# Chunked attention, top-2 routing and experts on one core: the attention as a four-stage pipeline, with the routing cut into single steps

## The chip, the cores and the metric

One Trainium2 chip, of which the kernel uses one core. The metric is the device time of one execution in microseconds. TensorE multiplies (PE in the profile, its weight loads PEld), VectorE is DVE, ScalarE is ACT, GpSimd is POOL, SyncE is SP. Each engine runs its own instructions in order and waits for others by semaphores. DMAs are issued by POOL, SP or ACT and run on 16 DMA engines of the core.

## The reference

Two steps. First attention over batches b = 0..3, 8 heads, 768 positions, head size 64: each chunk of 32 positions sees 16 positions to its left, its own 32, 8 to its right, and 8 memory positions:

```
k_full = concat([mem_k, k[l_start:r_end]]); v_full likewise
scores = (q_c @ k_full.T) / 8
a = softmax(scores)
out[chunk] = a @ v_full
```

Then the outputs, as 3072 tokens of 512 numbers, go through a mixture of 8 experts with noise on the routing:

```
noisy = x @ w_gate + log1p(exp(x @ w_noise)) * noise
top2, their softmax weights g
out[n] = sum over the two experts e of g * (relu(x @ w1[e]) @ w2[e])
```

## The kernel before, in words

**Attention.** A head pair n (0 to 15; four per batch) is two heads side by side on 64 partitions each. `load_group` (L253) fetches q, k and v for two pairs at once; there are eight such groups and three buffers. POOL issues the q, k and v DMAs (L261, L274 to L280); SP issues the memory rows of v (L282) and the blank rows of the scatter target (L87). For one pair:

- `qkT` (L333): TensorE transposes q and k in 12 steps of 128x128 f32 (L342), ACT casts them to bf16 (L343), POOL copies the edges of k by 16 and 8 columns (L344, L345), so that each chunk sees a window of 56 columns.
- `scores` (L348): 48 matmuls of a chunk's 32 queries with its 56 keys (L356), then 48 with the 8 memory keys (L362), on array tiles of 64x32; VectorE takes maximum and difference (L367, L369), ACT the exponential (L370).
- `probT` (L373): six transposes (L377) and a copy out of PSUM by VectorE (L379).
- `cast_v` (L285): v is cast to bf16 by POOL for even pairs and VectorE for odd ones (L290), with two edge chunks scaled (L292).
- `mix` (L384): 48 matmuls with v (L394), VectorE divides by the sum (L398, L399) into the batch's row buffer `xrow`, two of which take turns.

The loop (L406) runs `qkT(n+2)`, `probT(n)`, `scores(n+1)`, `mix(n)`, `cast_v(n+1)`. After each second `qkT` it asks for the group two further on.

**Routing.** `dispatch` (L126) follows each batch by one pair. For 6 tiles of 128 tokens it transposes the rows (L133), ACT copies them (L135), TensorE makes 16 logits (L137). Then some 35 small VectorE operations (L142 to L224) find the two best experts, the rank of each token in its pair of experts (with sums by TensorE, L173 to L177 and L191 to L195, over `seen` of the batches before) and its slot (L204). POOL scatters the rows to `x_by_pair` in DRAM in 6 indirect DMAs (L227). The routing of the last batch comes after the loop.

**Experts.** The 28 pairs of experts have 128 slots each. SP reads the rows back (L487, L490, L450) when all scatters have landed; POOL issues the expert weights (L437, L438; two experts' are buffered), TensorE does both matmuls (L512, L547), ACT and VectorE evict, POOL scatters the output (L554). A loop over spilled rows behind it runs only where a pair of experts got more than 128 tokens and 32 spill rows are used up.

**What sets the order.** The kernel's text gives a priority to each instruction, and a scheduler puts them in one fixed order per engine when the kernel is built, where it may move an instruction ahead of others that wait. What the order holds is therefore read from the built kernel; on each engine it is kept on the chip. PSUM has 8 banks: scores 2, transposes 3, mixes 2, routing 1.

Of the kernel before, what the change touches and what calls it, by code (L numbers as in the profile page):

```python
# [12 lines left out]
F32 = mybir.dt.float32  # L13
# [8 lines left out]
def kernel(  # L22
# [102 lines left out]

    def dispatch(b, xrow):  # L126
        T = lambda name, shape, dt=F32: rpool.tile(shape, dt, name=name)
        t0 = b * BT
        ps_l = psR.tile([128, BT, 2 * E], F32, name="ps_l", tag="rt")
        for t in range(BT):  # L130
            p_x = psT.tile([128, KP, 128], BF16, name="p_x", tag="tr")
            for kp in range(KP):
                nc.tensor.transpose(out=p_x[:, kp, :], in_=xrow[:, t, kp * 64:(kp + 1) * 64].bitcast(BF16), identity=identb)  # L133
            xt = rpool.tile([128, KP, 128], BF16, name="xt")
            nc.scalar.copy(xt, p_x)  # L135
            for kp in range(KP):
                nc.tensor.matmul(out=ps_l[:, t, :], lhsT=xt[:, kp, :], rhs=wgn[:, kp, :], start=(kp == 0), stop=(kp == KP - 1))  # L137
        ns = T("ns", [128, BT, E])
        nc.scalar.activation(out=ns, in_=ps_l[:, :, E:], func=Act.Exp)
        nc.scalar.activation(out=ns, in_=ns, func=Act.Ln, bias=1.0)  # L140
        nl = T("nl", [128, BT, E])
        nc.vector.tensor_mul(nl, ns, nz_all[:, t0:t0 + BT, :])  # L142
        nc.vector.tensor_tensor(out=nl, in0=nl, in1=ps_l[:, :, :E], op=Alu.add)

        codeb = code.rearrange("p (o e) -> p o e", o=1).to_broadcast([128, BT, E])
# [4 lines left out]
        for i, src in enumerate((nl, nl2)):  # L150
            nc.vector.tensor_reduce(out=m[i], in_=src, axis=AX, op=Alu.max)
            nc.vector.tensor_tensor(out=eq, in0=src, in1=bc(m[i], E), op=Alu.is_equal)
            nc.vector.tensor_mul(eq, eq, codeb)
            nc.vector.tensor_reduce(out=c[i], in_=eq, axis=AX, op=Alu.max)
            if i == 0:
                nc.vector.tensor_tensor(out=eq, in0=codeb, in1=bc(c[0], E), op=Alu.is_equal)
                nc.vector.scalar_tensor_tensor(out=nl2, in0=eq, scalar=-1e30, in1=nl, op0=Alu.mult, op1=Alu.add)

        cM, cm = T("cM", [128, BT]), T("cm", [128, BT])
        nc.vector.tensor_max(cM, c[0], c[1])  # L160
        nc.vector.tensor_tensor(out=cm, in0=c[0], in1=c[1], op=Alu.min)
        pa, pb, pos = T("pa", [128, BT]), T("pb", [128, BT]), T("pos", [128, BT])
        nc.vector.tensor_scalar(out=pa, in0=cM, scalar1=float(E - 1), scalar2=None, op0=Alu.mult)
        nc.vector.scalar_tensor_tensor(out=pa, in0=cm, scalar=-float(E), in1=pa, op0=Alu.mult, op1=Alu.add)
        nc.vector.tensor_scalar(out=pb, in0=cM, scalar1=-float(E), scalar2=float(E * E), op0=Alu.mult, op1=Alu.add)
        nc.vector.scalar_tensor_tensor(out=pb, in0=cm, scalar=float(E - 1), in1=pb, op0=Alu.mult, op1=Alu.add)
        nc.vector.tensor_tensor(out=pos, in0=pa, in1=pb, op=Alu.min)

        oh = T("oh", [128, BT, NB], BF16)
        nc.vector.tensor_tensor(out=oh, in0=ramp.rearrange("p (o e) -> p o e", o=1).to_broadcast([128, BT, NB]),  # L170
                                in1=bc(pos, NB), op=Alu.is_equal)
        ps_r = psR.tile([128, BT, NB], F32, name="ps_r", tag="rt")
        nc.tensor.matmul(out=ps_r, lhsT=upper, rhs=oh, start=True, stop=False)  # L173
        for t in range(1, BT):
# [3 lines left out]
                         start=False, stop=True)  # L178
        sums = T("sums", [128, NB])
        nc.vector.tensor_reduce(out=sums, in_=oh.rearrange("p t e -> p e t"), axis=AX, op=Alu.add)  # L180
        nc.vector.tensor_add(seen, seen, sums)

        rk = T("rk", [128, BT, NB])
        rank = T("rank", [128, BT])
        nc.vector.tensor_tensor(out=rk, in0=oh, in1=ps_r, op=Alu.mult)
        nc.vector.tensor_reduce(out=rank, in_=rk, axis=AX, op=Alu.add)

        ov = T("ov", [128, BT], BF16)
        nc.vector.tensor_scalar(out=ov, in0=rank, scalar1=float(CAP), scalar2=None, op0=Alu.is_ge)
        ps_o = psR.tile([128, BT + 1], F32, name="ps_ov", tag="rt")  # L190
# [4 lines left out]
        nc.tensor.matmul(out=ps_o[:, :BT], lhsT=ones, rhs=seen_ov.to_broadcast([128, BT]), start=False, stop=True)  # L195
        ov1 = T("ov1", [128, 1])
        nc.vector.tensor_reduce(out=ov1, in_=ov, axis=AX, op=Alu.add)
        nc.vector.tensor_add(seen_ov, seen_ov, ov1)
        slot, spl = T("slot", [128, BT]), T("spl", [128, BT])
        nc.vector.scalar_tensor_tensor(out=slot, in0=pos, scalar=float(CAP), in1=rank, op0=Alu.mult, op1=Alu.add)  # L200
        nc.vector.scalar_tensor_tensor(out=spl, in0=ps_o[:, :BT], scalar=float(NB * CAP), in1=slot, op0=Alu.add, op1=Alu.subtract)
        nc.vector.tensor_mul(spl, spl, ov)
        slot_i = rpool.tile([128, BT], I32, name="slot_i")
        nc.vector.tensor_tensor(out=slot_i, in0=slot, in1=spl, op=Alu.add)  # L204

        ex, g1, g2 = T("ex", [128, BT]), T("g1", [128, BT]), T("g2", [128, BT])
        nc.vector.tensor_sub(ex, m[1], m[0])
        nc.scalar.activation(out=ex, in_=ex, func=Act.Exp)
        nc.vector.tensor_scalar(out=g1, in0=ex, scalar1=1.0, scalar2=None, op0=Alu.add)
        nc.vector.reciprocal(g1, g1)  # L210
        nc.vector.tensor_mul(g2, ex, g1)
        first = T("first", [128, BT])
        nc.vector.tensor_tensor(out=first, in0=c[0], in1=c[1], op=Alu.is_gt)
        dg = T("dg", [128, BT])
        nc.vector.tensor_sub(dg, g1, g2)
        nc.vector.tensor_mul(dg, dg, first)

        meta = xrow[:, :, XC:].bitcast(F32)
        nc.vector.tensor_copy(meta[:, :, 0:1], tok_i[:, t0:t0 + BT].rearrange("p (t o) -> p t o", o=1))
        o1 = lambda ap: ap.rearrange("p (t o) -> p t o", o=1)  # L220
        nc.vector.tensor_tensor(out=meta[:, :, 1:2], in0=o1(g2), in1=o1(dg), op=Alu.add)
        nc.vector.tensor_tensor(out=meta[:, :, 2:3], in0=o1(g1), in1=o1(dg), op=Alu.subtract)
        nc.vector.tensor_copy(meta[:, :, 3:4], o1(cM))
        nc.vector.tensor_copy(meta[:, :, 4:5], o1(cm))  # L224
        nc.gpsimd.memset(meta[:, :, 5:8], 0.0)
        for t in range(BT):
            nc.gpsimd.indirect_dma_start(  # L227
                out=xd_tile[t0 + t], out_offset=bass.IndirectOffsetOnAxis(ap=slot_i[:, t:t + 1], axis=0),
                in_=xrow[:, t, :], in_offset=None, bounds_check=NROW - 1, oob_is_err=True)
        if b == B - 1:  # L230
            nc.tensor.matmul(out=ps_o[:, BT:BT + 1], lhsT=ones, rhs=seen_ov, start=True, stop=True, skip_group_check=True)
            nc.vector.tensor_copy(n_spill, ps_o[:, BT:BT + 1])
            nc.vector.tensor_scalar(out=n_spill_i, in0=ps_o[:, BT:BT + 1], scalar1=float(SPILL), scalar2=None, op0=Alu.max)


    actx = ExitStack()
    apool = actx.enter_context(tc.tile_pool(name="apool", bufs=2))
    psS = actx.enter_context(tc.psum_pool(name="psS", bufs=1))
    psT = actx.enter_context(tc.psum_pool(name="psT", bufs=3))
    psA = actx.enter_context(tc.psum_pool(name="psA", bufs=1))  # L240
    psR = actx.enter_context(tc.psum_pool(name="psR", bufs=1))
# [8 lines left out]
    PADL, PADR = left_ctx, right_ctx  # L250
# [34 lines left out]
    def cast_v(n):  # L285
# [3 lines left out]
        eng = nc.vector if n % 2 else nc.gpsimd  # L289
        eng.tensor_copy(vw[:, 1:ncnk - 1, 0:D], vf[:, hp % HV, 1:ncnk - 1, :])  # L290
        for c, col in ((0, live[:, 0:1]), (ncnk - 1, live[:, 1:2])):
            eng.tensor_scalar(out=vw[:, c, 0:D], in0=vf[:, hp % HV, c, :], scalar1=col, scalar2=None, op0=Alu.mult)  # L292
# [40 lines left out]
    def qkT(n):  # L333
        b, hp = divmod(n, HP)
        qn, kn, _ = groups_in[b, hp // HV]
        qT = apool.tile([128, S], BF16, name="qT", bufs=3)
        kT = apool.tile([128, PADL + S + PADR], BF16, name="kT", bufs=3)
        for src, dst, o in ((qn, qT, 0), (kn, kT, PADL)):
            for g in range(2):
# [3 lines left out]
                nc.scalar.copy(dst[:, o + g * HT * 128:o + (g + 1) * HT * 128], p_t)  # L343
        nc.gpsimd.tensor_copy(kT[:, :PADL], kT[:, PADL:2 * PADL])  # L344
        nc.gpsimd.tensor_copy(kT[:, PADL + S:], kT[:, S + PADL - PADR:S + PADL])  # L345
        st[n].update(qT=qT, kT=kT)

    def scores(n):  # L348
        b, hp = divmod(n, HP)
        qT, kT = st[n]["qT"], st[n]["kT"]  # L350
        ps = [psS.tile([128, BT, CTX], F32, name=f"ps_s{hh}") for hh in range(2)]
        for c in range(ncnk):
            u, r = divmod(c, 4)
            for hh in range(2):
                hs = slice(64 * hh, 64 * hh + 64)
                nc.tensor.matmul(out=ps[hh][32 * r:32 * r + 32, u, :WIN], lhsT=qT[hs, chunk * c:chunk * (c + 1)],  # L356
                                 rhs=kT[hs, chunk * c:chunk * c + WIN], start=True, stop=True)
        for c in range(ncnk):
            u, r = divmod(c, 4)
            for hh in range(2):  # L360
# [283 lines left out]
```

## Time and profile before

| | us |
|---|---|
| median of 3 timed runs (lowest, highest) | 483.78 (481.44, 484.1) |
| profiled execution | 479.79 |
| its span | 478.0 |
| TensorE busy in the span | 322.1 (67%) |
| VectorE, ACT, POOL busy | 171.6, 127.4, 165.2 |

A row of a timeline is: start in us from the span's start, duration in us, engine, line, operation, output<-inputs, shapes, count of instructions merged into the row, and in brackets the engine's idle time just before it with what ended it. "issue" there means that nothing the profile shows was waited for. A row of the windows is: from:to, length, then for PE, PEld, DVE, ACT, POOL the busy time and the number of instructions, then the granted TensorE clock as a share of full speed, the share of the time for which the DMA engines were busy, and the GB/s that they moved. "to landing" is the time from a DMA's issue to its completion.

### The profile page before, as it was taken

The numbers are of one execution on the slowest core, as the hardware profiler recorded it, in microseconds if no ns is written. First come the engines' busy times: TensorE is split into PE (matmuls) and PEld (weight loads), VectorE is DVE, ScalarE is ACT, GpSimd is POOL, SyncE is SP. The second block draws the span as 40 slices with busy tenths as digits, with TensorE's granted clock in tenths as the row PEclk, the third lists the DMA queues.
The fourth block names the chain that finished last, engine by engine and source line by source line (L and its number), as shares of the span: only waits on it lengthen the run. The fifth ranks groups of instructions, "written<-read, shape, count | busy, mean of one in ns | idle before, by whom it ended". The sixth has DMA issues, their size and how long they took to land. (4 is left out here: it accounts for less than half of the span.)

```text
span 478.0 us, 10565 instructions
## 1 busy us (share of the span) xinstructions
PE 322.1 (67%) x4481; PEld 199.1 (42%) x4497; DVE 171.6 (36%) x493; ACT 127.4 (27%) x233; POOL 165.2 (35%) x267
## 2 busy tenths in 40 slices
PE   2225555454555484510399599599899999999992
PEld 2114444344444363400254265264455545454541
DVE  1014437565346468440230231231324323333341
ACT  2212232623352244500033123132231223131200
POOL 9756562179317810651100100200303140313133
PEclk9999985965556566555599789899999999999998
DMA  7999998139922800299315615715835665761112
GB/s 136 261 294 282 293 224 178 48 99 209 237 55 86 203 6 3 71 191 226 86 33 90 121 36 88 137 30 88 172 61 123 100 148 87 161 110 73 40 57 86
DMA packets 41842, 60.06 MB, mean 126 GB/s; under 512 B 14170, under 2 KB 29623, under 8 KB 41792
## 3 DMA queue, kind: packets, MB, share of 16 engines
q0 software_dynamic: 23008, 49.93, 47.0%
q1 hardware_dynamic: 18464, 9.35, 8.9%
q8 instruction: 37, 0.61, 0.6%
q14 instruction: 13, 0.11, 0.1%
q10 hardware_dynamic: 320, 0.07, 0.1%
HBM read 62.73 MB, written 14.47 MB: 162 GB/s over the span
## 5 line engine op out<-in xcount | busy, mean ns | idle before, releaser
L512 PE MATMUL ps_h<-xTb,w1t 128*128 128x384 bf16 (+4 forms) x832 | 112.8, 292 | 1.0 <-DVE xTb L454 1.0
L547 PE MATMUL ps_y<-w2t,ht 128*128 128x512 bf16 x432 | 97.1, 379 | 0.9
L512 PEld LDWEIGHTS <-w1t 128*128 128x128 bf16 x832 | 62.0, 99 | 44.3 <-issue 3.7
L516 ACT ACTIVATE ht<-ps_h 128x512 bf16<-128x512 f32 x64 | 38.2, 597 | 133.6 <-PE ps_h L512 133.6
L547 PEld LDWEIGHTS <-ht 128*128 128x128 bf16 x448 | 43.2, 98 | 51.5
L518 DVE TENSOR_SCALAR ht<-ps_h 128x416 bf16<-128x416 f32 x64 | 37.9, 592 | 65.2 <-PE ps_h L512 65.2
L554 POOL DMA_INDIRECT out_dram<-acc,tid x28 | 28.1, 1003 | 78.4 <-DVE acc L553 41.0
L553 DVE SCALAR_TENSOR_TENSOR acc<-ps_y,meta,acc 128x512 f32<-128x512 f32 x28 | 21.0, 751 | 54.5 <-PE ps_y L547 54.5
L227 POOL DMA_INDIRECT x_by_pair<-xrow,slot_i x24 | 24.5, 1023 | 37.3 <-DVE vwin L292 15.1
L551 ACT ACTIVATE acc<-ps_y,meta 128x512 f32<-128x512 f32 x28 | 19.2, 687 | 61.3 <-PE ps_y L547 61.3
L342 PE MATMUL p_t<-ident,qn 128*128 128x128 f32 x96 | 22.5, 393 | 13.8 <-DMA qn<-in_q_dram 11.8
L370 ACT ACTIVATE P<-sd 128x384 bf16<-128x384 f32 x32 | 15.7, 522 | 54.4 <-DVE sd L369 54.4
L343 ACT CAST qT<-p_t 128x384 bf16<-128x384 f32 x32 | 15.1, 479 | 42.8 <-PE p_t L342 42.4
L356 PE MATMUL ps_s<-kT,qT 64*32 64x56 bf16 x768 | 13.9, 219 | 16.7 <-POOL kT L344 5.7
L437 POOL DMA_DIRECT2D w1t<-in_moe_w_dram x8 | 6.4, 801 | 54.1 <-PE ps_h L512 54.1
L280 POOL DMA_DIRECT2D vf<-in_v_dram x16 | 22.8, 1426 | 6.2 <-issue 5.6
L342 PE MATMUL p_t<-ident,kn 128*128 128x128 f32 x96 | 21.0, 380 | 5.6 <-DMA kn<-in_k_dram 5.6
L455 POOL COPY meta<-xl 128x8 f32<-128x8 f32 x28 | 5.3, 190 | 55.7 <-DMA xl<-x_by_pair 55.6
L367 DVE TENSOR_REDUCE mx<-ps_s 128x6 f32<-128x384 f32 x32 | 16.4, 550 | 21.6 <-PE ps_s L362 18.8
L453 PE MATMUL p_t<-identb,xl 128*128 128x128 bf16 x112 | 13.0, 250 | 15.3 <-DMA xl<-x_by_pair 10.5
L342 PEld LDWEIGHTS p_t<-ident,qn 128*128 128x128 f32 x96 | 16.3, 203 | 15.3 <-issue 12.5
L362 PE MATMUL ps_s<-mkT,qT 64*32 64x8 bf16 x768 | 10.4, 176 | 16.8 <-issue 16.8
(139 smaller groups left out, 379.3 us busy)
## 6 DMA issues: line engine op xcount, KB each, us to landing
vf<-in_v_dram POOLq DMA_DIRECT2D x14, 672.0 KB, 14.4
w1t<-in_moe_w_dram POOLq DMA_DIRECT2D x8, 1024.0 KB, 8.4
w2t<-in_moe_w_dram POOLq DMA_DIRECT2D x8, 1024.0 KB, 11.1
qn<-in_q_dram POOLq DMA_DIRECT2D x14, 384.0 KB, 11.8
kn<-in_k_dram POOLq DMA_DIRECT2D x14, 384.0 KB, 11.8
x_by_pair<-blank SPq DMA_DIRECT2D x1, 3696.0 KB
xl<-x_by_pair SPq DMA_DIRECT2D x28, 132.0 KB
vf<-in_mem_v_dram SPq DMA_DIRECT2D x32, 48.0 KB
```

The lines of the kernel that those rows point to most:

```text
L227: nc.gpsimd.indirect_dma_start(out=xd_tile[t0 + t], out_offset=bass.IndirectOffsetOnAxis(ap=slot_i[:, t:t + 1], axis=0), in_=xrow[:, t, :] ...
L280: nc.gpsimd.dma_start(out=dst[:, lo:hi, :], in_=src(lo, hi - lo))
L342: nc.tensor.transpose(out=p_t[:, t * 128:(t + 1) * 128], in_=src[:, hp % HV, g * HT + t, :, :], identity=ident)
L367: nc.vector.tensor_reduce(out=mx, in_=ps[hh], axis=AX, op=Alu.max)
L370: nc.scalar.activation(out=P[:, :, hh, :], in_=sd, func=Act.Exp, scale=scale)
L512: nc.tensor.matmul(out=ps_h[:, off:off + n], lhsT=w1t[:, kp, f * 128:(f + 1) * 128], rhs=rhs(kp), start=(kp == 0 and i == 0), stop=(kp == ...
L516: nc.scalar.activation(out=ht[:, f, lo:hi], in_=ps_h[:, :hi - lo], func=Act.Relu)
L518: nc.vector.tensor_scalar(out=ht[:, f, lo:hi], in0=ps_h[:, :hi - lo], scalar1=0.0, scalar2=None, op0=Alu.max)
L547: nc.tensor.matmul(out=ps_y, lhsT=ht[:, f, j * CAP:(j + 1) * CAP], rhs=w2t[:, f, :], start=(f == 0), stop=(f == FB - 1))
L551: nc.scalar.activation(out=acc[p], in_=ps_y, func=Act.Copy, scale=gate)
L553: nc.vector.scalar_tensor_tensor(out=acc[p], in0=ps_y, scalar=gate, in1=acc[p], op0=Alu.mult, op1=Alu.add)
L554: nc.gpsimd.indirect_dma_start(out=out_tile[p], out_offset=bass.IndirectOffsetOnAxis(ap=tid[p][:, 0:1], axis=0), in_=acc[p], in_offset=Non ...
```

## The change

It has six parts, all ahead of the experts.

- The loop is a pipeline of four stages: in step n, `qkT(n)`, `scores(n-1)`, `probT(n-2)` with `cast_v(n-2)`, `mix(n-3)`. A group is asked for as soon as the second `qkT` of the group three before it is through.
- `dispatch` is a generator. `tick()` runs it on to its next `yield`; it is called 10 times per pair, between the VectorE operations of the pair. A routing has 59 such steps and joins the list of jobs when its batch's last `mix` is through. What is left after the loop is run off there.
- POOL issues DMAs only: the 56 columns of the edge chunks are made by two matmuls each (`context`) in place of the copied edges of k, and v is cast by ACT for every pair, its edges scaled by VectorE. The column of zeros in the row buffer is set once, at the start.
- There are three row buffers, made once, in place of two.
- In the scores the context matmul and the memory matmul of a chunk and head stand one behind the other, where there were 48 and then 48.
- PSUM: 3 banks for transposes and all routing results, 5 shared by scores and mixes. The six tiles' logits are copied out to `lg` one by one, and the copies of the transposed rows are shared by VectorE and ACT.

The diff, cut to its core (the many `V.` lines of the routing are the same operations as before, with a `yield` between them, some in another order):

```diff
     def dispatch(b, xrow):
...
         for t in range(BT):
             p_x = psT.tile([128, KP, 128], BF16, name="p_x", tag="tr")
             for kp in range(KP):
                 nc.tensor.transpose(...)
-            xt = rpool.tile([128, KP, 128], BF16, name="xt")
-            nc.scalar.copy(xt, p_x)
+            yield
+            xt = rpool.tile([128, KP, 128], BF16, name="xt", bufs=3)
+            (nc.scalar.copy if t % 2 else V.tensor_copy)(xt, p_x)
+            yield
+            ps_l = psT.tile([128, 2 * E], F32, name="ps_l", tag="tr")
             for kp in range(KP):
-                nc.tensor.matmul(out=ps_l[:, t, :], ...)
+                nc.tensor.matmul(out=ps_l, ...)
+            yield
+            V.tensor_copy(lg[:, t, :], ps_l)
+            yield
...
+    def tick(n=1):
+        for _ in range(n):
+            while jobs:
+                try:
+                    next(jobs[0])
+                    break
+                except StopIteration:
+                    jobs.pop(0)
...
-    psS = actx.enter_context(tc.psum_pool(name="psS", bufs=1))
     psT = actx.enter_context(tc.psum_pool(name="psT", bufs=3))
-    psA = actx.enter_context(tc.psum_pool(name="psA", bufs=1))
-    psR = actx.enter_context(tc.psum_pool(name="psR", bufs=1))
+    psW = actx.enter_context(tc.psum_pool(name="psW", bufs=5))
...
     def cast_v(n):
-        eng = nc.vector if n % 2 else nc.gpsimd
-        eng.tensor_copy(vw[:, 1:ncnk - 1, 0:D], vf[:, hp % HV, 1:ncnk - 1, :])
+        nc.scalar.copy(vw[:, 1:ncnk - 1, 0:D], vf[:, hp % HV, 1:ncnk - 1, :])
         for c, col in ((0, live[:, 0:1]), (ncnk - 1, live[:, 1:2])):
-            eng.tensor_scalar(...)
+            V.tensor_scalar(...)
...
     def qkT(n):
...
-        nc.gpsimd.tensor_copy(kT[:, :PADL], kT[:, PADL:2 * PADL])
-        nc.gpsimd.tensor_copy(kT[:, PADL + S:], kT[:, S + PADL - PADR:S + PADL])
...
     def scores(n):
-        ps = [psS.tile([128, BT, CTX], F32, name=f"ps_s{hh}") for hh in range(2)]
+        ps = [psW.tile([128, BT, CTX], F32, name="ps_s", tag="w") for _ in range(2)]
         for c in range(ncnk):
             for hh in range(2):
-                nc.tensor.matmul(out=ps[hh][32 * r:32 * r + 32, u, :WIN], lhsT=qT[hs, ...], rhs=kT[hs, ...], ...)
-        for c in range(ncnk):
-            for hh in range(2):
-                nc.tensor.matmul(out=ps[hh][32 * r:32 * r + 32, u, WIN:], lhsT=qT[hs, ...], rhs=mkT[hs, ...], ...)
+                for a, z, t in context(kT, hs, c):
+                    nc.tensor.matmul(out=o[:, a:z], lhsT=ql, rhs=kT[hs, t:t + z - a], start=True, stop=True)
+                nc.tensor.matmul(out=o[:, WIN:], lhsT=ql, rhs=mkT[hs, hp, b * n_mem:(b + 1) * n_mem], ...)
...
+    for i in range(3):
+        xr = rcon.tile([128, BT, ROW], I32, name=f"xrow{i}")
+        nc.gpsimd.memset(xr[:, :, XC:], 0)
...
+        if hp == HP - 1:
+            jobs.append(dispatch(b, xrows[b % 3]))
...
-    qkT(0)
-    qkT(1)
-    scores(0)
-    cast_v(0)
-    for n in range(NPAIR):
-        b, hp = divmod(n, HP)
-        if n + 2 < NPAIR:
-            qkT(n + 2)
-        if (n + 2) % HV == HV - 1 and (n + 2) // HV + 2 < len(GR):
-            load_group(*GR[(n + 2) // HV + 2])
-        probT(n)
-        if n + 1 < NPAIR:
-            scores(n + 1)
-        mix(n)
-        if n + 1 < NPAIR:
-            cast_v(n + 1)
-        if n == 0:
-            fill_blank()
-        if hp == 0 and b > 0:
-            dispatch(b - 1, xrows[b - 1])
-    dispatch(B - 1, xrows[B - 1])
+    for n in range(NPAIR + 3):
+        if n < NPAIR:
+            qkT(n)
+            if n % HV == HV - 1 and n // HV + 3 < len(GR):
+                load_group(*GR[n // HV + 3])
+        tick()
+        if 0 <= n - 1 < NPAIR:
+            scores(n - 1)
+        if 0 <= n - 2 < NPAIR:
+            probT(n - 2)
+            cast_v(n - 2)
+        if 0 <= n - 3 < NPAIR:
+            mix(n - 3)
+        if n == 2:
+            fill_blank()
+    while jobs:
+        tick()
```

## The prediction

> **What bounds the kernel now.** The page's chain of waits is of no use here: it stops after one piece, the last output DMA. So I read the table of windows first, cut where the stages change, then the timelines of POOL, of TensorE and of the hand-over to the experts. The profiled execution took 479.79 us, its span 478.0; the median of the three timed runs is 483.78, 4.0 us more. I work in the profiled execution and carry the difference to the median at the end.
>
> The windows, with each engine's busy time, the granted clock, the share of DMA time and GB/s:
>
> ```profile
> 37.00:82.00 45.00, 23.91 (x863) 19.88 (x863) 22.69 (x51) 12.08 (x28) 23.81 (x35) 0.84 1.02 253
> 82.00:126.00 44.00, 23.26 (x719) 19.36 (x716) 24.30 (x87) 17.18 (x37) 26.54 (x33) 0.66 0.57 137
> 126.00:170.00 44.00, 21.98 (x591) 18.78 (x588) 21.00 (x78) 15.36 (x31) 21.36 (x30) 0.54 0.50 120
> 170.00:195.00 25.00, 16.62 (x581) 12.86 (x581) 19.43 (x83) 11.87 (x23) 2.94 (x7) 0.64 0.02 4
> ...
> 237.40:478.00 240.60, 218.89 (x1615) 114.70 (x1628) 70.93 (x124) 57.46 (x92) 46.92 (x87) 0.95 0.45 92
> ```
>
> The experts start at 237.4 us and keep TensorE busy for 218.9 of 240.6 us. The change touches nothing there, so I carry that stage unchanged and look only at when it starts. Ahead of it no engine is over 60% busy, and DMA is full only until 82 us. Two things waste the time. First, POOL's queue is in order, and a scatter that waits for its slots holds up the loads behind it:
>
> ```profile
> 88.72 1.11 POOL L261 DMA_DIRECT2D qn<-in_q_dram  x1 [0.16 <-issue]
> 96.72 1.24 POOL L227 DMA_INDIRECT x_by_pair<-xrow,slot_i  x1 [6.89 <-DVE vwin L292]
> ...
> 104.38 1.10 POOL L261 DMA_DIRECT2D qn<-in_q_dram  x1
> ```
>
> The load begun at 88.72 goes on at 104.38, 14.6 us after its first part ended; the same happens at 135.53 (on at 152.72). The last group's loads thus leave POOL at 159.3. Second, TensorE, when it has work, stands still with no releaser:
>
> ```profile
> 44.66 0.26 PE L362 MATMUL ps_s<-mkT,qT 64*32 64x8 bf16 x20 [2.64 <-issue]
> ...
> 52.50 0.24 PE L356 MATMUL ps_s<-kT,qT 64*32 64x56 bf16 x6 [3.03 <-issue]
> ...
> 59.18 0.25 PE L356 MATMUL ps_s<-kT,qT 64*32 64x56 bf16 x16 [2.61 <-issue]
> ```
>
> In the packed trace each of these stops holds one 16 KB packet of the instruction queue (37 packets in all), and they lie 256 TensorE instructions apart: code loading, 2.8 us each while DMA is full. Last, the hand-over: the last routing block's slots, its last scatter, the first read of the scattered rows, the first expert matmul:
>
> ```profile
> 208.73 0.16 DVE L204 TENSOR_TENSOR slot_i<-slot,spl 128x6 int32<-128x6 f32 x1
> ...
> 216.22 0.98 POOL L227 DMA_INDIRECT x_by_pair<-xrow,slot_i  x1 [0.30 <-issue]
> ...
> 228.18 0.32 SPq L487 DMA_DIRECT2D s_x<-x_by_pair  x1
> ...
> 237.46 1.06 PE L512 MATMUL ps_h<-xTb,w1t 128*128 128x512 bf16 x2
> ```
>
> I call T the end of the last pair's sd on VectorE, 190.5 us (L369). From T to the experts there are 47 us.
>
> **Part by part.** I price T' (T in the changed kernel), then the tail from T'.
>
> *POOL issues only.* The kT edge copies (32 at 0.2 us) and half the V casts (8 at 1.37 us and 16 edges at 0.44) leave POOL. In the built order all five remaining load groups stand ahead of the first scatter, each waiting only for its buffers. So the 14.6 and 16.1 us holes go. What is late next? The bytes: eight groups of 3.07 MB (0.77 q, 0.77 k, 1.34 v, 0.19 memory rows) and 3.7 MB of blanks, 28.3 MB; at the 253 GB/s of 37 to 82 us that is 112 us. Two pairs behind the last landing T' would be about 128: the floor.
>
> *V cast on ACT.* The trace has no such cast. ACT's rows 128x384 (479 ns) and 128x512 (597) give 118 ns per 128 columns, so 128x1408 takes about 1.4 us (VectorE 0.89, POOL 1.37 for the same): 16 of them 23 us on an ACT that is busy 56.5 of the 158 us from 37 to 195. It waits for vf, behind it the next pairs' qT casts; the vf of a group lands before the q of the next, so I charge nothing; the bound is one vf landing, 13.8 us (median), once.
>
> *VectorE.* 16 more edge scalings (0.25), 12 xt copies (0.42, as L454's equal shape), 24 logit copies (0.16), less 8 casts (0.89): +5.8 us on 87.4 busy of 158. Hidden beside TensorE.
>
> *TensorE's own work.* Busy from 37 to 195 us: 85.8 us. Of that the changed order puts before 32 us (scores of pairs 0 and 1, no longer queued behind pair 2's transposes) 1.9 us, and behind T' routing 2 (4.9, as the window of 195 to 217 has for routing 3), the end of routing 1 (1.3) and the last two pairs' transposes and mixes (2.9). Left: 74.8 us. The granted clock fell to 0.54 without making this work longer per matmul (27.7 ns a matmul in 37:82, 28.6 in 170:195), so I take it as it stands.
>
> *Code loading* is not removed: the instruction number stays (64 matmuls more). Between 42 and 195 us the trace has 22 packets; some 19 fall between 32 us and T'. About 12 of them come while the loads still fill DMA, at 2.8 to 3 us: 35 us. The other 7 at some 0.7 us (in 170:195, with DMA empty, TensorE stops of that kind are below 1.3 us): 5 us. The Trainium skill (Runtime: NRT & Kernel Launch, Instruction fetch mechanics) calls the crossing of a 16 KiB block "mostly hidden". By that T' would fall to the DMA floor; the three rows above speak against it where DMA is full.
>
> *The pipeline and the five shared PSUM buffers.* L356 x43 then x5 shows the scores waiting for their single buffer; with five, softmax is taken from a pair earlier. I take these waits as gone but for 3 us.
>
> T' = 32 (k of pairs 2 and 3 arrives at 31.8, L342) + 74.8 + 40 + 3 = **150**.
>
> *Routing spread out.* One step is made per tick: 59 steps per routing, 10 ticks per pair. So a routing takes almost six pairs, four routings need 236 ticks, and from the first routing on the loop has only 111. The rest is drained after the last pair. The built VectorE order shows it: after the last sd come the second half of routing 1, the multiplications of the last four pairs (they wait for scatter 0 to free the row buffer), all of routing 2, then all of routing 3. From T':
> - end of routing 1: second selection to slots 6.2 us (89.45 to 95.64), two PT copies and edges 1.7: 7.9
> - three tiles of routing 2's logits 3, four multiplications 2.2, mixes of 14 and 15 3.4: 16.5
> - rest of routing 2: logits 2.5, exp, table load and log 1.8 (199.55 to 201.34), chain 7.5 (201.35 to 208.9): 28.3
> - routing 3: logits 4.5 (195.03 to 199.5) and six copies 1, then 1.8 and 7.5: 43.1
> - six scatters 8.4 (slots to 217.2), landing 2.9: 54.4
> - first read to first matmul 9.3 (228.18 to 237.46): 63.7.
>
> Before, the scatter had landed only at 228, 11 us after its issue, beside four weight loads issued at 201 to 205. Now three of these are issued at about T'+17 and, at some 8 us each (8.4 and 11.1 to landing), are in by T'+45, so I take the 2.9. The bound is those 8 us again.
>
> So the tail grows from 47 to 64, +17; T falls by 40.5. Sum: -23.5 us. 479.8 - 23.5 = 456.3 in the profiled execution, 460.3 against the median; I say **458**.
>
> **The rivals.**
> *A, code loading is hidden after all* (loads come earlier and smoother, so its packets pass): T' = 128 + 6 for the last routing steps, experts at 198, 440 against the profile. For it: 9 of 22 packets cost nothing in the trace; against it: those nine came while TensorE waited for something else.
> *B, slower: two score matmuls in a row on one array tile.* The changed loop issues, for each chunk and head, the context matmul and at once the memory matmul on the same 64x32 tile; now 48 of one kind run over eight tiles in turn. The order is not in the trace. Below: nothing (96 in 0.95 us from 37.25 to 38.20, 10 ns each, L356 and L362). Above: as L193, five on one tile in 0.27 us, 54 ns each: 48 x 44 ns = 2.1 us per pair, 14 pairs, +30: 486. It decides from 1.6 us per pair, where the 23.5 us are used up. I take nothing, since operand shapes are those of L356 and L362, but keep the end. The Trainium skill (TensorEngine Tiling (Array Packing), Tiling Modes) says that different tiles can load and multiply in parallel, which promises nothing for one tile twice.
> *C, it doesn't do what it says:* the pairs keep nearly their pace (11 us per pair from 82 to 170) because code loading and in-order waits for routing steps fill the holes. Of the 40 us T loses only 15 to 22: 474 to 482. For it: TensorE busy plus 2.9 us per packet is already 39 of every 44 us.
>
> **Chances.** Forecast 0.56 (own range 446 to 470: 12 packets at 2 to 4 us, weights in the way or not); A 0.14; B 0.12; C 0.14; other 0.04. The range leaves out B and the far ends of A and C: 438 to 480. A measurement here tells about 0.5%, 2.4 us. Faster by more: forecast, A, most of C: 0.80. Within: 0.06. Slower: B and a little of C: 0.14.
>
> **What would show it.** Right: POOL's loads without the 15 us holes, the last group issued near 100 us; T' near 150 with TensorE stops of 2 to 4 us and no releaser, most before 110; two routings one behind the other between the last mix and the last scatter, some 27 us; experts near 214, then 240 us as before. Wrong: a T' near 130 (A), score blocks of over 2.5 us per pair (B), T' past 170 (C), or an expert stage of another length.

## The result, and the profile of the changed kernel

The changed kernel takes 507.08 us (median of 4 runs, 504.0 to 515.7), the kernel before 482.61 in the same comparison: 1.0495 of it, 95% interval 1.041 to 1.058. It is slower, by about what it was forecast to gain, and outside the range. The profiled execution is the slowest of the four, 515.7 us with a span of 513.9, so its rows hold some 9 us more than the median; a second profile (below), of 513.8 us, has the same rows.

First the windows, 10 to 60 us, while loads fill DMA in both kernels (columns as in the prediction: PE, PEld, DVE, ACT, POOL, clock, DMA share, GB/s). Before:

```profile
10.00:60.00 50.00, 20.22 (x517) 16.38 (x518) 12.14 (x30) 11.12 (x25) 31.21 (x38) 1.00 1.08 277
```

After:

```profile
10.00:60.00 50.00, 19.40 (x558) 15.78 (x558) 10.69 (x25) 13.09 (x24) 23.31 (x24) 0.89 1.08 215
```

DMA is as busy (1.08) and moves 22% less. The page's list of DMA issues (KB each, median us from issue to landing) says the same. Before, these loads landed after 14.4 us (v) and 11.8 (q and k); now:

```profile
vf<-in_v_dram POOLq DMA_DIRECT2D x14, 672.0 KB, 21.5
...
qn<-in_q_dram POOLq DMA_DIRECT2D x14, 384.0 KB, 19.9
kn<-in_k_dram POOLq DMA_DIRECT2D x14, 384.0 KB, 21.6
```

Next SP's queue. The memory rows of v for pairs 4 and 5 (the `x4`) are issued behind the blank write (L87). Before, SP is through with them at 62.9 us:

```profile
9.26 0.66 SPq L87 DMA_DIRECT2D x_by_pair<-blank  x1
9.96 52.95 SPq L282 DMA_DIRECT2D vf<-in_mem_v_dram  x4
```

After, at 97.9:

```profile
10.24 2.90 SPq L87 DMA_DIRECT2D x_by_pair<-blank  x1
13.19 84.68 SPq L319 DMA_DIRECT2D vf<-in_mem_v_dram  x4
```

Who waits for these rows is in the timelines of ACT, TensorE and POOL:

```profile
114.46 2.63 ACT L326 CAST vwin<-vf 128x1408 bf16<-128x1408 f32 x2 [33.14 <-DMA vf<-in_mem_v_dram]
```

```profile
58.08 0.19 PE L402 MATMUL ps_s<-mkT,qT 64*32 64x8 bf16 x1 [6.41 <-issue]
...
85.65 0.50 PE L441 MATMUL ps_o<-vwin,PT 64*32 64x65 bf16 x34 [6.85 <-issue]
...
117.53 0.90 PE L378 MATMUL p_t<-ident,kn 128*128 128x128 f32 x3 [29.27 <-ACT qT L379]
...
132.58 0.19 PE L402 MATMUL ps_s<-mkT,qT 64*32 64x8 bf16 x1 [7.91 <-issue]
```

```profile
117.54 2.81 POOL L317 DMA_DIRECT2D vf<-in_v_dram  x2 [24.37 <-DMA vf<-in_mem_v_dram]
...
143.90 2.81 POOL L317 DMA_DIRECT2D vf<-in_v_dram  x2 [19.06 <-ACT kT L379]
```

ACT stands 33 us at the V cast of pair 4, the casts of q and k wait behind it, and TensorE and then POOL wait for those. The other three PE rows are stops with an instruction packet in them: 6.4 to 7.9 us, where the three rows of this kind in the prediction have 2.6 to 3.0. They stand inside blocks of scores and mixes whose first matmuls are already through. The hand-over, from DVE, POOL, SP and PE in turn:

```profile
211.15 0.55 DVE L412 TENSOR_TENSOR sd<-ps_s,mx 128x384 f32<-128x384 f32 x1
...
253.81 0.17 DVE L250 TENSOR_TENSOR slot_i<-slot,spl 128x6 int32<-128x6 f32 x1
```

```profile
260.75 0.98 POOL L254 DMA_INDIRECT x_by_pair<-xrow,slot_i  x1 [0.30 <-issue]
```

```profile
263.44 0.32 SPq L534 DMA_DIRECT2D s_x<-x_by_pair  x1
```

```profile
272.60 1.49 PE L559 MATMUL ps_h<-xTb,w1t 128*128 128x512 bf16 x3
```

T' (end of the last sd) is 211.7 us, not 150; from there the experts start 60.9 us later (forecast: 63.7) and take 241.3 (before: 240.5). So the whole miss lies ahead of T'. The table adds up the time from 32 us to T'. TensorE's idle stretches of over 1 us are sorted by whether an instruction packet falls into them (packed trace); shorter ones count as other waits.

| us | before | prediction | after | e13, load buffers moved (below) |
|---|---|---|---|---|
| start | 32 | 32 | 32 | 32 |
| TensorE's own work | 84.5 | 74.8 | 75.4 | 73.6 |
| stops with an instruction packet | 33.0 | 40 | 52.7 | 37.7 |
| the stop behind ACT's V cast | none | 0 | 29.3 | 11.2 |
| all other waits | 41.6 | 3 | 22.3 | 16.0 |
| end of the last sd | 191.1 | 150 | 211.7 | 170.5 |

### The profile page after: what moved, and what is told of

Same layout as the page of the kernel before. It is cut to its first block, busy times and chain, and to the rows that moved or that the text cites. A ratio compares the mean times of both kernels' runs of the same rounds, so it can differ in the third digit from the quotient of the medians.

```text
span 513.9 us, 10712 instructions
## 1 busy us (share of the span) xinstructions
PE 322.8 (63%) x4561; PEld 198.2 (39%) x4561; DVE 171.3 (33%) x537; ACT 142.9 (28%) x237; POOL 138.5 (27%) x210
## 5 line engine op out<-in xcount | busy, mean ns | idle before, releaser
L378 PE MATMUL p_t<-ident,kn 128*128 128x128 f32 x96 | 23.1, 392 | 48.9 <-ACT qT L379 41.1
L378 PEld LDWEIGHTS p_t<-ident,kn 128*128 128x128 f32 x96 | 16.8, 204 | 52.0 <-ACT qT L379 43.3
L326 ACT CAST vwin<-vf 128x1408 bf16<-128x1408 f32 x16 | 21.0, 1359 | 36.2 <-DMA vf<-in_mem_v_dram 33.1
L378 PE MATMUL p_t<-ident,qn 128*128 128x128 f32 x96 | 23.7, 415 | 10.7 <-DMA qn<-in_q_dram 10.7
L402 PE MATMUL ps_s<-mkT,qT 64*32 64x8 bf16 x768 | 18.6, 173 | 17.3 <-issue 17.3
L401 PE MATMUL ps_s<-kT,qT 64*32 64x56 bf16 (+3 forms) x832 | 20.5, 202 | 13.1 <-issue 11.9
L441 PE MATMUL ps_o<-vwin,PT 64*32 64x65 bf16 x768 | 11.8, 219 | 23.8 <-issue 23.8
L402 PEld LDWEIGHTS <-qT 64*32 64x32 bf16 x768 | 15.6, 100 | 19.5 <-issue 19.1
L298 POOL DMA_DIRECT2D qn<-in_q_dram x18 | 18.1, 1006 | 17.6 <-PE p_t L378 10.3
```

Of the source, the lines that this page charges most:

```text
L326: nc.scalar.copy(vw[:, 1:ncnk - 1, 0:D], vf[:, hp % HV, 1:ncnk - 1, :])
L378: nc.tensor.transpose(out=p_t[:, t * 128:(t + 1) * 128], in_=src[:, hp % HV, g * HT + t, :, :], identity=ident)
L401: nc.tensor.matmul(out=o[:, a:z], lhsT=ql, rhs=kT[hs, t:t + z - a], start=True, stop=True)
L402: nc.tensor.matmul(out=o[:, WIN:], lhsT=ql, rhs=mkT[hs, hp, b * n_mem:(b + 1) * n_mem], start=True, stop=True)
```

## The experiments

These are the theories, in the order in which they came. Theory 1: the memory rows of v come late because they stand behind the blank write, and the cast's place on ACT makes it worse. Theory 2: code loading in a full DMA is the loss. Theory 3, after the second profile: the load packets themselves got slower. In the packed trace the mean load packet takes 202 ns in the first 10 us before the change and, in the second profile, 299 after it, at the same size (304 in the first profile); over the first 60 us it is 204 against 262 to 266. What differs is where the packets go. In the built kernels q's first buffer starts at byte 52,224 of a partition before (102 x 512) and at 60,352 after (117 x 512 + 448). The third row buffer takes 6,336 bytes, a third xt and the new lg 1,792, together 8,128; 1,792 is 7 x 256, so the row buffer alone moves the rest off the multiples of 256. The buffers of q, k and v are multiples of 512 long, so all nine start 448 bytes behind a line of 512.

**a0_again**: the changed kernel once more.

> The changed kernel once more, for a second profile. Both theories: 502 to 509 us, and in the trace the same stop of ACT at the V cast of pair 4 (L326), 33 us in the first profile, ended by the landing of the memory rows of v (L319). If that stop is below 15 us here, the first profile's stop was an accident of that execution and the blank-queue theory loses its main row.

513.81 us, one run; ACT's stop at L326 34.2 us. As expected but for 5 us in the time.

**e1_blank_late**: the blank write behind the memory rows, asked for at `n == 12` in place of `n == 2`.

```
+ nc.vector.tensor_scalar(out=blank[:, 0:1].bitcast(F32), in0=late[:, 0:1], scalar1=0.0, scalar2=0.0, ...)   # late: mx of pair 11
```

> The 3.7 MB blank write (L87) is made to wait for pair 11's maximum, so that all 32 memory-row DMAs of v stand ahead of it in SP's queue; nothing else is changed. Theory 1 (memory rows of v behind the blank write; ACT's in-order cast waits 33 us for them, the casts of q and k queue behind it, TensorE stands 30 us): ACT's wait at L326 falls below 5 us and the time by 25 to 35 us against the changed kernel, to 472 to 482 us. Theory 2 (TensorE's code loading takes 5 to 8 us a packet while DMA is full, and that alone makes the pairs late): the bytes are only moved, code loading stays as long, the gain is below 10 us, 497 or more.

488.06 us, 1.014 (1.005 to 1.024). In this kernel the blanks come behind the first batch's scatter and overwrite its rows; the work done is the same. ACT's wait is gone (0.8 us at most), T' is 180.5. But load packets take 312 ns over the first 60 us, and at 488 it stays 6 us above what theory 1 gave.

**e2_cast_back**: the V cast and its edge scalings back on POOL and VectorE.

```
- nc.scalar.copy(vw[:, 1:ncnk - 1, 0:D], vf[...])
+ eng = nc.vector if n % 2 else nc.gpsimd
+ eng.tensor_copy(vw[:, 1:ncnk - 1, 0:D], vf[...])
```

> The V cast goes back to POOL for even pairs and VectorE for odd ones, with its edge scalings; all else as changed. Theory 1 in its simple form (rows late, whoever casts): rows land as late, near 114 us; ACT no longer waits, but TensorE reaches pair 4's mix within about two pairs and stops there, so the gain is 5 to 15 us: 492 to 502. Rival (the cast's place in ACT's queue is what turns late rows into a loss, since ACT feeds TensorE's transposes): the gain is the whole stop, 25 to 33 us: 474 to 482. Second rival: POOL's casts hold back the loads again as before, no gain: 505 or more.

506.53 us, 1.050 (1.042 to 1.058): nothing won, as the second rival's figure has it. The waits (us in total, times, longest) show that the stop moved on:

```profile
DVE vwin L329 <- DMA vf<-in_mem_v_dram: 34.1, 1, 34.1
...
POOL vwin L327 <- DMA vf<-in_mem_v_dram: 21.5, 1, 21.5
```

VectorE and POOL now stand for the same rows, with the pairs behind the one and the next loads behind the other; which of the two holds up the pairs is not separated. With rows this late it doesn't matter which engine casts.

**b_late3**: the same delay of the blank write in the kernel before (pair 3).

> The kernel before with the blank write made to wait for pair 3's maximum, behind the memory rows of the first four groups. Theory 1: the kernel before lost only about 5 us to these rows (its TensorE and ACT did not stop for them longer), so the time falls by 0 to 8 us: 475 to 484. Theory 2 (full DMA sets code loading): the DMA in the first 70 us is relieved by 3.7 MB, some 15 us of it, and TensorE's stops shrink: -8 to -15 us, 468 to 475.

484.40 us, 1.005 (1.002 to 1.009): no gain, rather a loss of 0.5%. In that kernel the place behind the blank write is no cost (in the changed kernel it is one, also with fast loads: see e5_align_blank). Theory 2 in this form is out too: the blanks were issued only at 62.4 us, and nothing got faster.

**e1_blank_mid**: the delay in the changed kernel by pair 8, ahead of the first scatter.

> The blank write made to wait for pair 8's maximum, ahead of the first scatter, in the changed kernel with its buffers where the change put them. Theories 1 and 3 agree that the stop at L326 goes: below 5 us, 478 to 490 us; packets stay at 300 ns. What is above 478 is then the slower loads themselves.

500.23 us, 1.037 (1.030 to 1.043), above both theories. The stop is gone, and yet only 7 us are won: T' is 190.4, where e1_blank_late has 180.5. The blanks, issued at 123.1 us, now run beside the last loads, which fits but is not tested further. The window shows what stays; no blanks are in it at all:

```profile
10.00:60.00 50.00, 18.56 (x558) 15.10 (x557) 10.51 (x25) 13.01 (x24) 22.59 (x24) 0.88 1.07 176
```

DMA is full and moves 176 GB/s. (With the blanks as late and the buffers on a border, in e5_align_blank below, it moves 231 in the same window.)

**e4_align, e4_again, e4_half, e13_half_again**: the changed kernel with an unused tile ahead of the load buffers, and nothing else.

```
+ pad = rcon.tile([128, 16], F32, name="pad")      # 64 bytes: byte 0 of 512; [128, 80], 320 bytes: byte 256
+ nc.vector.memset(pad, 0.0)
```

> The changed kernel with one unused tile of 64 bytes a partition ahead of the load buffers, and nothing else: the third row buffer and the rest of the change had put the buffers of q, k and v on byte 448 of a 512-byte line of SBUF (before: on byte 0); the 64 bytes put them back on 0. Theory 3 (written after the second profile of the changed kernel, whose load packets take 300 ns where the kernel before has 200, from the first 10 us on): packets fall to about 200 ns, the rows of pair 4's v land near 75 us where it was 114, ACT's wait at L326 falls from 34 to below 10 us and the time to 460 to 478 us. Theory 1 alone (the place behind the blank write): ACT waits over 20 us still, 495 or more. If the packets stay at 300 ns, the address has nothing to do with it.

> The changed kernel with 320 unused bytes instead of 64: the load buffers start on byte 256 of a 512-byte line. The rows of q, k and v that a descriptor writes are 256 bytes long. If 256-byte borders count (a row that starts 192 bytes behind one touches two 256-byte pieces), packets are at 200 to 240 ns as with byte 0 and the time is 484 to 490 us, as with 64 bytes. If only byte 0 of 512 counts, packets stay near 300 ns and the time is 500 us or more.

> The changed kernel with 64 unused bytes once more, as e4_align (487 us, where 320 bytes gave 476). If the 10 us between them come from the address, 484 to 489 again; if they are a drift between the two calls, 474 to 479, and then the changed order of the score matmuls costs nothing either (e8_split 477).

> The changed kernel with 320 unused bytes, as e4_half (476 us, 0.987 of the kernel before in its call). If the address makes the 10 us against the 64 bytes, 0.98 to 0.995 of the kernel before again; if the calls differ, 1.00 to 1.015 as with 64 bytes.

With 64 bytes the times are 486.85 us, 1.011 (1.007 to 1.016), and 487.86, 1.005 (1.002 to 1.009); with 320 bytes 476.28, 0.987 (0.983 to 0.992), and 475.82, 0.987 (0.983 to 0.991). Load packets take 194 to 199 ns in the first 60 us in all four. The window of e13_half_again:

```profile
10.00:60.00 50.00, 25.68 (x720) 21.15 (x720) 15.37 (x39) 19.85 (x36) 29.46 (x30) 0.66 1.08 287
```

and SP's queue, where pair 4's rows are out at 58.3 us in place of 97.9:

```profile
9.74 1.12 SPq L87 DMA_DIRECT2D x_by_pair<-blank  x1
10.90 47.42 SPq L321 DMA_DIRECT2D vf<-in_mem_v_dram  x4
```

An unused tile of 64 or 320 bytes wins 19 to 31 us. Byte 256 does as well as byte 0 for the packets, so lines of 512 are not what counts. Borders of 256 bytes, the length of a row of q, k and v, fit all runs; borders of 128 would too, and no run separates the two. The Trainium skill (DMA: Bandwidth & Descriptors, How a descriptor splits into AXI transactions) says that a transfer starting between borders of 256 bytes is begun at the border below it. By its count a row starting 192 bytes behind such a border takes 14 beats for 8, an estimate of 1.75 times; measured is 299 against 202 ns, 1.48, in the first 10 us and 1.3 over the first 60. The page tells it of reads; here only the side written into SBUF moved. e4_align missed its 460 to 478 us by 9: ACT still waits 12.1 us at the V cast, where I expected less than 10, and T' is 174.6. e4_half is 8 us below the 484 to 490 that I gave it. The 10 us between 64 and 320 bytes come again in the second comparison, so they belong to the programs; they lie in T' (2 to 6), the hand-over (4 to 6) and the experts (1 to 2). One place can be seen: the last mixes. e4_again makes four or five matmuls every 1.4 us:

```profile
189.92 0.26 PE L443 MATMUL ps_o<-vwin,PT 64*32 64x65 bf16 x4 [0.51 <-issue]
...
191.34 0.27 PE L443 MATMUL ps_o<-vwin,PT 64*32 64x65 bf16 x5 [1.16 <-issue]
```

In e13_half_again they run through:

```profile
182.25 0.97 PE L443 MATMUL ps_o<-vwin,PT 64*32 64x65 bf16 x72
```

But this stop does not go with the address of the load buffers. e1_blank_mid, with its buffers 448 bytes behind a line, has it too, and e8_split (below), with 64 unused bytes, has not:

```profile
203.74 0.27 PE L443 MATMUL ps_o<-vwin,PT 64*32 64x65 bf16 x5 [1.15 <-issue]
205.17 0.28 PE L443 MATMUL ps_o<-vwin,PT 64*32 64x65 bf16 x5 [1.16 <-issue]
```

Where it stands, the last mix ends 17 us behind T', elsewhere at most 12.7. What brings it about stays open.

**b_shift**: the reverse, 448 unused bytes in the kernel before.

> The kernel before with one unused tile of 448 bytes a partition, so that its q, k and v buffers start on byte 448 of a 512-byte line as in the changed kernel. Theory 3: packets take 300 ns, DMA moves about 175 GB/s where it moved 253, the first 82 us get some 25 us longer and the last groups 5 to 10: 500 to 515 us. Rival (the packets of the changed kernel are slow for another reason, such as three groups of loads in flight): packets stay at 200 ns and the time within 3 us of the kernel before.

517.71 us, 1.075 (1.068 to 1.081), 36 us lost and 3 us above the range I gave; packets take 286 ns in the first 10 us. Its window is like that of the changed kernel:

```profile
10.00:60.00 50.00, 16.04 (x340) 12.50 (x339) 8.85 (x20) 9.18 (x20) 27.60 (x33) 1.00 1.08 218
```

Three groups in flight, the order of the pairs and the third row buffer as such are out as causes of the slow packets: none of them is in this kernel. So the address alone costs the kernel before more than the whole change cost, and theory 3 holds in both directions.

**e7_noload**: what code loading costs without loads. Pairs 6 to 15 read the buffers of earlier groups, so their outputs are not the reference's.

```
- load_group(*GR[n // HV + 3])
+ groups_in[GR[n // HV + 3]] = groups_in[GR[n // HV]]
```

> As aligned and with the late blank write, but groups 3 to 7 aren't loaded: their pairs read the buffers of groups 0 to 2 again (the loads of q, k, v and memory rows of pairs 6 to 15 are left out). DMA is full only to about 45 us and during the blank write. Theory: code-loading stops of 3 to 7 us belong to full DMA, so behind 50 us they shrink to below 1.3 us each outside the blank write, and the last pair's sd comes at 125 to 140 us where it was 169. Rival: the stops belong to TensorE's own order or to the length of code, and stay at 3 to 5 us: sd above 155.

433.40 us, one run; the last sd at 129.5 us. TensorE's waits from 55 to 130 us that nothing in the profile ends, in e5_align_blank (the same kernel with its loads):

```profile
PE ps_o L445 <- issue: 16.6, 3, 6.8
PE ps_s L404 <- issue: 8.7, 2, 4.8
PE ps_s L405 <- issue: 6.6, 2, 5.1
```

and here:

```profile
PE ps_o L445 <- issue: 3.0, 4, 1.4
...
PE ps_s L405 <- issue: 0.7, 1, 0.7
PE ps_s L404 <- issue: 0.3, 1, 0.3
```

That is 31.9 us against 4.0. The stops belong to full DMA; without it the longest is 1.4 us, a shade over the 1.3 expected. The Trainium skill's "mostly hidden" (Runtime: NRT & Kernel Launch, Instruction fetch mechanics) fits this kernel and not the others.

**e8_split**: 64 bytes, and the scores issued in two halves as before.

> The changed kernel with aligned buffers and the scores issued as before: first all context matmuls, then all memory matmuls. Rival B of the prediction (two matmuls in a row on one tile cost up to 2.1 us a pair, 30 us) would give 457 to 480 us; if the order costs nothing, 484 to 490, as with 64 bytes alone.

476.69 us, 0.993 (0.990 to 0.997). The time fits rival B, the trace doesn't. Where no stop falls into it, a block of some 100 score matmuls takes 0.98 us with this order (131.7 us) and 0.98 with the changed one (e4_again, 130.5 us), and 1.05 for 96 before. B priced 2.1 us a pair; it is nothing. The time is that of the 320 bytes with the changed order, so it is the same open 10 us: the last mixes run through here.

**e12_align_back**: 64 bytes, and the V cast back on POOL and VectorE (theory 4: ACT's cast costs its wait also with fast loads).

> 64 unused bytes, and the V cast back on POOL and VectorE. Theory 4: ACT's cast of pair 4's v waits about 12 us for its rows also with aligned buffers and holds up the casts of q and k behind it, as the prediction's bound for this step had it (13.8 us, once); undone, 5 to 12 us are won against e4_again. Rival: as with unaligned buffers (e2_cast_back, no gain), VectorE and the mix wait as long: within 4 us of e4_again or slower, since POOL's casts again stand between its loads.

481.10 us, 0.985 (0.977 to 0.993), 7 us below e4_again. That is theory 4's figure, but the trace puts the gain elsewhere. T' is 175.9, in e4_again 176.5; the experts start 61.4 us behind T' in place of 66.9, and the last mixes, in another order here, end 5 us behind T' and not 17. POOL stands 12.2 us for the rows where ACT did. So it is not shown that the cast's place on ACT costs anything.

**e5_align_blank, e6_two_steps, e14_two_half**: towards a faster version. 64 bytes with the blank write behind pair 8's maximum; then pair 5 and `tick(n=2)`; then that with 320 bytes.

> Both edits: 64 bytes ahead of the load buffers and the blank write after pair 8's maximum. Theory 3 with 1: no wait at L326, packets 200 ns, T' at 150 to 160, 455 to 468 us, faster than both kernels. If code loading (3 to 8 us a packet in the changed kernel) does not shorten with the packets, T' stays above 170: 475 or more.

> Aligned buffers, the blank write after pair 5's maximum, and two routing steps per tick in place of one, so that a routing takes about three pairs and only the last batch's routing is left behind the last pair. By the tail's terms on record the routing 2 block (some 12 us) leaves the tail, and VectorE steps between the pairs cost 0 to 3 us: 462 to 470 us, against 477 with one step per tick. Rival: twice as many routing steps in order between the pairs' own instructions hold the pairs up as much as the tail gains: 474 or more.

> e6_two_steps (blank write after pair 5's maximum, two routing steps per tick) with 320 unused bytes in place of 64. If byte 256 is worth 10 us here too, 460 to 464 us; if not, 468 to 474. Against the kernel before 0.96 to 0.985 in any case.

The times are 477.28 us, 0.986 (0.980 to 0.991); 471.25, 0.980 (0.975 to 0.985); and 470.61, 0.977 (0.973 to 0.981). The first two miss their figures by 9 and 1 us. Against e4_align, which differs by the place of the blank write alone, e5 wins 9.6 us (5.5 between the two profiles, all of it ahead of T'), and ACT's longest wait at the V cast falls from 12.1 to 1.3 us: the late rows cost something with fast loads too. In e5 the stops with an instruction packet still sum to 45 us ahead of T' (169.1). In e6 the slots of routing 2 come at T' + 13.9 instead of T' + 30, but T' doesn't move and those of routing 3 come 32 us behind T'. e14 is faster than both kernels, by 2.3% of the kernel before; of the 10 us between 64 and 320 bytes less than 2 show in it, and neither e6 nor e14 has the slow last mixes.

**e10_four, e9_cast_early**: are POOL's waits for v buffers the limit (theory 5)? e6 with `bufs=4` for vf; e6 with `cast_v(n - 1)` right after `scores(n - 1)`.

> e6_two_steps (aligned, blank write after pair 5, two routing steps per tick) with four v buffers in place of three. Theory 5: POOL's waits at the v loads of the last three groups (13.1, 16.7 and 13.7 us in e6_two_steps, for buffers that ACT's casts and the mixes free late) go, the q and k loads behind them come 10 to 15 us sooner, the last sd moves from 170 to 150 to 160: 455 to 463 us. Rival: DMA is full up to 110 us anyway and code loading then takes longer: above 467.

> e6_two_steps with v cast right after the same pair's scores, one pair sooner, three v buffers. Theory 5: each v buffer comes free one pair (8 to 10 us) sooner, POOL's waits shrink by as much, 460 to 466 us. Rival: the cast waits for v that lands later than the scores are ready and holds up ACT: 470 or more.

480.82 us, 0.991 (0.987 to 0.995), and 480.41, 0.989 (0.984 to 0.994), neither faster than e6 (0.980). With four buffers the waits at v's loads from 70 us on are under 3 us but for the last group's, and T' is 178.7 all the same; with the early cast they stay at 14 and 16 us. Theory 5 has nothing for it. What e10 does show fits its rival: the stops with an instruction packet sum to 45.1 us ahead of T', in e6 to 38.8. Whether the pairs hang on these buffers is therefore not settled; a fourth buffer doesn't help.

## Why the prediction was wrong

The step that failed is T' = 150, and in it first the carrying over of DMA's speed. The 253 GB/s of 37 to 82 us, the code packets at 2.8 to 3 us and the vf landing of 13.8 us are rows of the kernel before and hold for its buffers' addresses. With the new addresses a full DMA moves 215 GB/s from 10 to 60 us where it moved 277. The change gives memory to a third row buffer; I counted its instructions and DMAs, not what moves behind it. b_shift and the four padded kernels show it from both sides: with the buffers on the border 19 to 31 us go, where the change had cost 24.5.

That is not all of the miss: 476 to 488 us is still 18 to 30 above the 458. This rest lies in two terms of T' that were put at nothing or nearly so, the wait at the V cast and the other waits, and with 64 bytes also in the open stop of the last mixes.

Point by point:

- **Code loading, 40 us**: right in kind, 12.7 too small with the slow packets, 37.7 once the address is mended. That the sum then fits is partly luck: the prediction had 12 stops of 2.8 to 3 us and 7 short ones, e13_half_again has 9 of 2.7 to 6.5 us. e7_noload shows that the stops come with full DMA.
- **V cast on ACT, nothing**: the step said that "the vf of a group lands before the q of the next". I had looked at POOL's loads of v and passed over SP's memory rows, which write into the same buffer and stand behind 3.7 MB of blanks. It cost 29.3 us in the changed kernel; with the address mended TensorE waits 11.2, within the bound that I gave and didn't use. Earlier rows win 5 to 10 us of it back (e5 against e4_align); another engine for the cast wins nothing in time (e2) or ahead of T' (e12).
- **Other waits, 3 us**: by the same count the kernel before has 41.6. I took nearly all of them as gone without pricing them; 22.3 stayed, and 16 with the address mended. The split into x43 and x5 that I read as a wait for the buffer is an order (transposes stand between); the wait before the x43 is 1.2 us. What the 16 us are is not settled.
- **POOL's holes go**: those at scatters went, and others of 24, 19, 14 and 13 us came at v's loads, the first for the late rows, the rest for a buffer. e10, which takes such holes away but for the last, wins nothing.
- **TensorE's work** (74.8, measured 75.4), **the tail** (63.7, measured 60.9; slots of routing 2 at T' + 25.7 for 28.3, of routing 3 at + 42.3 for 43.1) and **the experts** came out as worked out. (T, given as 190.5, is the start of the last sd; it ends at 191.1. That moves the sum by less than half a microsecond.)
- **Rival A** is false: code loading isn't hidden while loads fill DMA. **B** has the right sign by another mechanism; its own price is zero. The 0.27 us of five matmuls from which it was priced (L193) include the 0.17 that a single one takes (L195). **C** (474 to 482, pairs keep nearly their pace) is what the change does once its buffers lie right: 476 to 488.

So the change without the accident of the address comes to -1.3% to +1.1%: T' falls by 15 to 21 us, and the drained routings, with the open stop of the last mixes in some of the kernels, give 15 to 20 back.

## What to carry to other kernels

When a change adds or resizes a buffer, compare the addresses of all DMA targets before and after: nothing else of a load needs to change for its packets to take 1.3 to 1.5 times as long. The DMA share of the profile shows no difference; only GB/s at the same share does. An unused tile of a few bytes ahead of the buffers is the cheapest test, and it belongs into both kernels. In-order queues turn one late transfer into a stop of every engine behind it, so a cast is only free if each DMA that writes its input is early, whichever queue issues it.

## What the runs showed that I had not expected

- Load packets of rows of 256 bytes take 202 ns in the first 10 us with targets on a border of 256 bytes and 299 with targets 192 bytes behind one; from 10 to 60 us DMA moves 277 to 287 against 215 to 218 GB/s at a share of 1.08.
- Instruction packets compete with loads: from 32 us to T' TensorE's stops with one in them are up to 1.4 us without loads (55 to 130 us), 2.7 to 6.5 us in e13_half_again with fast load packets (the one behind the cast left out), and 2.7 to 8.5 us in the second profile of the changed kernel.
- An issue on SP can itself last: the four memory-row DMAs behind the 3.7 MB write took SP 52.95 us to issue before and 84.68 after (the first of the four 35.4 and 58.4), and every memory row behind them waits for that.
